# Cluster-ordered attention for the last batch of a routing-attention and PReLU feed-forward kernel

## The chip, the cores and the metric

One core of one Trainium2 chip runs the whole kernel. The metric is device microseconds of an execution, the median of three runs. Engines: TensorE (PE; PEld loads its weights), VectorE (DVE), ScalarE (ACT), GpSimd (POOL), SyncE (SP, which here only issues DMAs).

## The reference

```python
batch, n_heads, seq, head_dim = (4, 8, 768, 64); n_clusters = 16
q_assign = argmax(q_n . c_n);  k_assign = argmax(k_n . c_n)      # per head
mask = q_assign[:, :, :, None] == k_assign[:, :, None, :]
scores = where(mask, q @ k.T / sqrt(D), -1e9)
attn = softmax(scores)                                           # fp32
x = (attn @ v) as (B*S, H*D) = (3072, 512)
h = x @ w_in                                                     # (512, 2048)
g = maximum(h, 0) + alpha * minimum(h, 0)                        # alpha per column, random in 0..0.3
out = g @ w_out                                                  # (2048, 512)
```

A query attends only to keys of its own cluster. w_in, w_out and alpha arrive as 64-bit floats and are converted on the chip. Everything else is fp32.

## The kernel before, in words

**Tiling.** Two heads of a batch form a pair n (4 pairs a batch, 16 in all), a half is 384 of the 768 queries. Keys come in 6 chunks of 128. A step is one third of (pair, half): 3 steps a half, 12 for the four pairs of a half (UB), 96 in all (NS). The order is batch, half, pair.

**Attention.** `load` (L105) and `load_v` (L127) fetch a pair, in 32-element blocks, so that `prep_blocks` (L346) can turn it with VectorE block transposes into features by tokens. `prep_sims` (L362, TensorE) and `prep_argmax` (L372, VectorE) find the cluster of each token, `prep_clusters` and `prep_queries` (L407, L432) spread it into the layout that the mask needs. `score` (L470) multiplies each key chunk with the half's 384 queries for both heads: the two heads use 64 rows of the array each and run side by side (L484). ScalarE takes exp (L502, L505), and `mask` (L513) multiplies by "query's cluster equals key's cluster" with a VectorE operation of two inputs. Batch 0 is masked by an extra matmul instead. `add_up`, `turn`, `rows_sums`, `total` and `invert` (L523 to L569) build the softmax denominators: sums over chunks and a block transpose on VectorE, then a tiny matmul (L551) and a reciprocal. `weigh` (L571) multiplies values with E (L594), the two heads in two column halves; `normalise` (L617) writes xT, features by tokens.

**Feed-forward.** `ffn_pieces` (L628) cuts a half of a batch into 28 pieces: 16 `hidden` (four matmuls of 384 columns, L645, then two Relus on ScalarE, L652 and L653, and one VectorE operation L637) and 12 `final` (four matmuls of 512 columns, L665). The y of three token tiles are added on VectorE (L673) or copied on ScalarE (L671) and leave by SP (L676).

**Order.** The program order is written out by hand; each engine runs its own instructions in that order and waits for the others' semaphores. From step 24 on (L793) a step consists of slots. At the first step of a half, `score`, `invert`, `weigh` and `normalise` of the half before come first; then each slot runs one entry of `todo` (masks, sums), some feed-forward pieces of the half of a batch whose attention is complete (`feed`), and what `prep_at` has put there. `later(k, ...)` runs a piece k slots on. At the end the queue of pieces is emptied (L860): the feed-forward of the last half of batch 3 has no attention beside it. One piece is held back (L813, L837) to lie under the last `normalise`.

**Buffers.** The loads use `inp`, four tiles; small matmul results use one PSUM bank (`misc`, L79); feed-forward results and the two heads of a lone score chunk use two PSUM banks of `ps_f`; the exponentials have 9 E tiles after `more_room` (L465), which reuses the conversion's raw tiles. Weights are converted in steps up to 24, with GpSimd operations (L264). After that GpSimd has nothing to do.

**Check and slow path.** At the end a flag tells whether the softmax, which subtracts no maximum, stayed in range (L847 to L862). If not, `general` computes everything again. With these inputs it isn't run.

Of the kernel before, what the change touches and what calls it, by code (L numbers as in the profile page):

```python
# [8 lines left out]

FP32 = mybir.dt.float32  # L10
BF16 = mybir.dt.bfloat16
U32 = mybir.dt.uint32
# [9 lines left out]
def kernel(  # L22
# [21 lines left out]
    SCALE = float(D) ** -0.5  # L44
    GROUP = 2
# [16 lines left out]
    raws = fast.enter_context(tc.tile_pool(name="raws", bufs=1))  # L62
    cvt = fast.enter_context(tc.tile_pool(name="cvt", bufs=3))
# [5 lines left out]
    tpool = fast.enter_context(tc.tile_pool(name="tpool", bufs=2))  # L69
# [5 lines left out]
    fast.enter_context(tc.manual_schedule())  # L75

# [22 lines left out]
    pairs = [(b, hp) for b in range(B) for hp in range(NCH)]  # L99
    NP = len(pairs)  # L100
# [109 lines left out]
    def prepare_constants():  # L210
# [5 lines left out]
        for h in range(2):  # L216
# [7 lines left out]
        alpha_neg = const.tile([P, NF], FP32, name="alpha_neg")  # L224
        nc.vector.tensor_scalar(out=alpha_neg, in0=aps[:, 0:NF], scalar1=-1.0,
                                scalar2=None, op0=ALU.mult)
        return cT, alpha_neg
# [144 lines left out]
    def prep_argmax(n, ps):  # L372
# [15 lines left out]
        nc.vector.tensor_reduce(out=first, in_=top, axis=AX.X, op=ALU.max)  # L388
        firsts[n] = first
        if n >= NCH:  # L390
            return
        nc.vector.tensor_tensor(
            out=top, in0=top, in1=first[:, :, None].broadcast_to((P, 2 * NX, NC)),
            op=ALU.is_equal)
        member = fsp.tile([P, 2, HS], BF16, name="member")
# [36 lines left out]
    def prep_queries(n, half, h):  # L432
# [3 lines left out]
        if n < NCH:  # L436

            if h == 0:
# [12 lines left out]

    SB = NJ // GROUP
    assert NJ == GROUP * SB and SB == GT
    steps = [(b * NCH + hp, half, s)
             for b in range(B) for half in range(2)
             for hp in range(NCH) for s in range(SB)]
    NS = len(steps)
# [6 lines left out]

    def more_room():  # L465
        for raw in raw_tiles:
            e_tiles.insert(0, raw.rearrange("p n w -> p (n w)").bitcast(FP32)[
                :, 0:2 * HS].rearrange("p (h q) -> p h q", h=2))

    def score(n, half, chunks, alone=None):  # L470
# [7 lines left out]
        def bank(ps, h):  # L478
            return (ps[h] if isinstance(ps, list) else ps[:, h, :])[:, 0:HS]

        for c, ps in zip(chunks, pss):
            for h in range(2):
                r = h * D
                nc.tensor.matmul(  # L484
                    out=bank(ps, h),
                    lhsT=qkT[r:r + D, S + c * P:S + (c + 1) * P],
                    rhs=qkT[r:r + D, half * HS:(half + 1) * HS], start=True,
                    stop=not early_mask)
# [528 lines left out]
```

## Time and profile before

| | |
|---|---|
| time, median of 3 runs | 1021.64 us (1021.16 to 1021.64) |
| profiled execution | 1021.76 us, span 1019.6 us, clock 0.996 |
| DVE, busiest group L518 (masks) | 88.6 + 71.2 us |
| POOL after 175 us | nothing |
| DMA | 43.09 MB, mean 42 GB/s |

A group's row gives the line, engine and operation, out<-in by the program's names, partitions x elements, type and count; then the busy time in all, the mean ns of one, and the idle time just before them with the engine and line that ended it. A matmul row starts with the rows*columns of the array that it uses. An fp32 matmul of the source is two records. Two matmuls on different halves of the array overlap, and busy time counts the overlap once. The rows of stretches give start:end, length, then for each engine its busy time and count, the granted clock of TensorE, the DMA share and GB/s.

### The profile page before, as it was taken

How to read it: one execution, taken by the hardware profiler on the slowest of the kernel's cores; microseconds unless marked ns; L12 is line 12 of the kernel's file. 1: busy time of each engine (PE TensorE's matmuls, PEld its weight loads, DVE VectorE, ACT ScalarE, POOL GpSimd, SP SyncE). 2: the span in 40 equal slices, each digit the busy share in tenths (PEclk: the TensorE clock that was granted, in tenths of full speed). 3: DMA queues.
4: the chain of work that ended last, by engine and by line, in shares of the span. 5: the costliest groups of instructions: out<-in, count | busy, mean ns of one | idle time of the engine just before them, and what ended most of it. 6: DMA issues, size and time to landing. Idle time of an engine off the chain costs nothing.

```text
span 1019.6 us, 10615 instructions
## 1 busy us (share of the span) xinstructions
PE 998.6 (98%) x4067; PEld 491.3 (48%) x4067; DVE 671.5 (66%) x1185; ACT 325.0 (32%) x620; POOL 50.4 (5%) x71
## 2 busy tenths in 40 slices
PE   8899999999999999999999999999999999999997
PEld 5434444444454544545454454545445454544453
DVE  5887798588474776868667665878856585762111
ACT  5655544223230323313132232313323141321120
POOL 2323222000000000000000000000000000000000
PEclk9999999999999999999999999999999999999999
DMA  6533664030000232040000240213000000000000
GB/s 246 195 106 107 150 140 46 16 78 1 0 1 21 41 47 47 1 85 8 1 1 11 52 47 16 31 37 57 1 0 1 32 1 0 1 11 21 1 0 34
DMA packets 106122, 43.09 MB, mean 42 GB/s; under 512 B 95360, under 2 KB 98896, under 8 KB 106064
## 3 DMA queue, kind: packets, MB, share of 16 engines
q1 hardware_dynamic: 105216, 41.95, 18.0%
q8 instruction: 34, 0.56, 0.2%
q10 hardware_dynamic: 848, 0.39, 0.2%
q14 instruction: 24, 0.20, 0.1%
HBM read 35.69 MB, written 6.29 MB: 41 GB/s over the span
## 4 chain that ended last, share of the span: by engine, by line
PE 91%; DVE 4%; ACT 2%; DMA 1%; issue 1%; POOL 0%; ACTq 0%; DVEq 0%; POOLq 0%
PE fps L665 32%; PE fps L645 32%; PE vps L594 11%; PE sps L484 9%; PE fps L484 4%; PE mps L366 1%; PE sps L494 1%; ACT E L505 1%; ACT member L400 1%; DMA aq<-member 1%; PE mps L551 0%; ACT power L252 0%; PE fps L339 0%; PE fps L587 0%; DVE gT L637 0%
## 5 line engine op out<-in xcount | busy, mean ns | idle before, releaser
L645 PE MATMUL fps<-xT,w_in_sb 128*128 128x384 f32 x1024 | 342.4, 490 | 0.0
L665 PE MATMUL fps<-w_out_sb,gT 128*128 128x512 f32 x768 | 337.9, 595 | 1.1 <-DVE gT L637 1.1
L645 PEld LDWEIGHTS fps<-xT,w_in_sb 128*128 128x128 f32 x1024 | 190.8, 190 | 141.3 <-ACT raw L502 4.9
L665 PEld LDWEIGHTS fps<-w_out_sb,gT 128*128 128x128 f32 x768 | 143.9, 190 | 174.0 <-issue 161.1
L652 ACT ACTIVATE gT<-fps 128x384 f32<-128x384 f32 x128 | 62.9, 491 | 272.6 <-PE fps L645 272.6
L637 DVE SCALAR_TENSOR_TENSOR gT<-neg,alpha_neg,gT 128x384 f32<-128x384 f32 x128 | 80.6, 636 | 100.2 <-ACT neg L653 99.5
L518 DVE SCALAR_TENSOR_TENSOR raw<-aq,key,raw 128x384 f32<-128x384 bf16 x160 | 88.6, 613 | 35.0 <-ACT raw L505 23.1
L484 PE MATMUL sps<-qkT 64*128 64x384 f32 x576 | 110.9, 504 | 0.7 <-ACT E L505 0.7
L505 ACT ACTIVATE E<-sps 128x768 f32<-128x768 f32 x88 | 67.2, 813 | 71.4 <-PE sps L494 42.2
L518 DVE SCALAR_TENSOR_TENSOR E<-aq,key,E 128x384 f32<-128x384 bf16 x128 | 71.2, 613 | 19.2 <-ACT E L505 12.8
L594 PE MATMUL vps<-E,vt 128*64 128x384 f32 x448 | 82.9, 498 | 0.0
L484 PEld LDWEIGHTS sps<-qkT 64*128 64x128 f32 x576 | 52.0, 188 | 52.2 <-issue 20.9
L529 DVE TENSOR_TENSOR acc<-acc,E 128x768 f32<-128x768 f32 x64 | 61.2, 956 | 17.1 <-ACT E L505 15.3
L673 DVE TENSOR_TENSOR y<-y,fps 128x512 f32<-128x512 f32 x30 | 20.6, 686 | 74.5 <-PE fps L665 74.5
L653 ACT ACTIVATE neg<-fps 128x384 f32<-128x384 f32 x128 | 62.0, 484 | 0.1
L505 ACT ACTIVATE raw<-sps 128x768 f32<-128x768 f32 x56 | 42.9, 813 | 55.3 <-PE sps L484 55.2
L671 ACT COPY y<-fps 128x512 f32<-128x512 f32 x24 | 14.1, 586 | 135.5 <-PE fps L665 135.5
L594 PE MATMUL vps<-raw,vt 128*64 128x384 f32 x320 | 56.5, 491 | 0.0
L594 PEld LDWEIGHTS vps<-E,vt 128*64 128x64 f32 x448 | 29.6, 138 | 41.4 <-issue 41.1
L529 DVE TENSOR_TENSOR acc<-acc,raw 128x768 f32<-128x768 f32 x48 | 45.9, 955 | 1.0
L484 PE MATMUL fps<-qkT 64*128 64x384 f32 x192 | 41.5, 508 | 0.0
L502 ACT ACTIVATE raw<-fps 128x384 f32<-128x384 f32 x48 | 21.0, 493 | 59.2 <-PE fps L484 59.2
(99 smaller groups left out, 618.9 us busy)
## 6 DMA issues: line engine op xcount, KB each, us to landing
raw<-in_moe_w_in_dram SPq DMA_DIRECT2D x16, 512.0 KB, 4.5
raw<-in_moe_w_out_dram SPq DMA_DIRECT2D x16, 512.0 KB, 3.6
vt<-in_v_dram SPq DMA_DIRECT2D x16, 384.0 KB, 4.3
out_dram<-y SPq DMA_DIRECT2D x24, 256.0 KB, 2.0
qk<-in_q_dram SPq DMA_DIRECT2D x48, 96.0 KB, 3.8
qk<-in_k_dram SPq DMA_DIRECT2D x48, 96.0 KB, 3.6
qk<-in_q_dram SPq DMA_DIRECT2D x4, 384.0 KB, 5.4
qk<-in_k_dram SPq DMA_DIRECT2D x4, 384.0 KB, 5.9
```

The lines of the kernel that those rows point to most:

```text
L484: nc.tensor.matmul(out=bank(ps, h), lhsT=qkT[r:r + D, S + c * P:S + (c + 1) * P], rhs=qkT[r:r + D, half * HS:(half + 1) * HS], start=True, ...
L502: nc.scalar.activation(out=E[:, h, :], in_=ps[h][:, 0:HS], func=AF.Exp, scale=SCALE)
L505: nc.scalar.activation(out=E, in_=ps[:, :, 0:HS], func=AF.Exp, scale=SCALE)
L518: nc.vector.scalar_tensor_tensor(out=E[:, h, :], in0=aqs[n, half][:, h, :], scalar=keys[n][:, NJ + c, h:h + 1], in1=E[:, h, :], op0=ALU.is ...
L529: nc.vector.tensor_tensor(out=acc, in0=acc if first is None else first[3], in1=E, op=ALU.add)
L594: nc.tensor.matmul(out=po[r:r + D, 0:HS], lhsT=vts[n][:, h, c, :], rhs=e[:, h, :], start=(c == 0), stop=(c == NJ - 1))
L637: nc.vector.scalar_tensor_tensor(out=gs[f], in0=neg, scalar=alpha_neg[:, f:f + 1], in1=gs[f], op0=ALU.mult, op1=ALU.add)
L645: nc.tensor.matmul(out=ps[:, 0:HS], lhsT=w_in_sb[:, c, f * P:(f + 1) * P], rhs=xT[:, c, :], start=(c == 0), stop=(c == NCH - 1))
L652: nc.scalar.activation(out=gs[f], in_=ps[:, 0:HS], func=AF.Relu)
L653: nc.scalar.activation(out=neg, in_=ps[:, 0:HS], func=AF.Relu, scale=-1.0)
L665: nc.tensor.matmul(out=ps[:, 0:DM], lhsT=gs[f][:, i * P:(i + 1) * P], rhs=w_out_sb[:, f, :], start=on and f == f0, stop=off and f == f0 + ...
L673: nc.vector.tensor_tensor(out=ys[i], in0=ys[i], in1=ps[:, 0:DM], op=ALU.add)
```

## The change

- The last batch (n = 12 to 15) is no longer done in halves; its pairs take three steps each, so 84 steps instead of 96 (`steps += [(n, None, s) ...]`).
- Ahead of that, at steps 30, 36, 54 and 60 (`ORDERS`), a pair's queries and keys are loaded and turned, their clusters found (`order_sims`, `order_counts`), each token's running number in its cluster counted with a scan, and its place in cluster order worked out (`order_begins`, `order_ranks`).
- One entry a slot (`sorting`), q, k and v of 64 tokens at a time go through a stage tile and are scattered by GpSimd's indirect DMA as rows of 512 bytes to DRAM, q and, apart from them, k beside v, in cluster order: 12 scatters a head, 24 a pair, and 18 loads of stage tiles by SP. The token's number goes along with q. `order_load` reads the sorted rows back, four steps before use.
- In cluster order, a key chunk c is multiplied only with the query tiles c-1, c and c+1 (`window`). The sums over chunks (`add_near`), the weighing (`weigh_near`) and the masks take the same windows. The second half's product uses the misc bank.
- Way back: `normalise_near` writes features by sorted tokens; six TensorE transposes (`to_rows`) give rows, 12 indirect DMAs a pair put rows of 256 bytes to their tokens' places in DRAM (`put_back`), `fetch_back` reads them in blocks and `turn_back` turns them into xT, all spaced by slots.
- Both halves of the last batch's feed-forward follow at the end; 4 pieces are held back at the end of the steps 60 to 71 and 10 at the end of 72 to 83 (`kept`).
- PReLU: one ScalarE copy, then VectorE's max(alpha * h, h), in place of two Relus and h+ - alpha * h-. This holds for alpha up to 1, which is tested at the end.
- Also at the end: a test that each cluster's queries lie within the windows; if one fails, `general` runs.
- Memory: the conversion's tiles are freed at step 24 (`second_part`), five E tiles, the order's tiles and a third xT tile take their place. The sorted blocks, the tile before the way back and the one after it all come from `inp`'s four tiles.

```diff
+    def order_features(n, w):
+        us[n, w] = inp.tile([P, 2, NJ, D], FP32, name="qk").rearrange("p h j d -> p (h j d)")
+        nc.vector.transpose(out=us[n, w],
+                            in_=raw_qk.pop((n, w)).rearrange("p h j d -> p (h j d)"))
...
+        top, first = argmax(ps)
+        only_first(top, first)
+        member = ordp.tile([P, HS], BF16, name="mine")
+        nc.vector.transpose(out=member, in_=top.rearrange("p t c -> p (t c)"))
+        count = asg.tile([P, HS], FP32, name="simT")
+        nc.vector.tensor_tensor_scan(count, member, member, 0.0, ALU.add, ALU.max)
+        us[n] = member, count
+    def order_begins(n):
+        member, count = us[n]
+        ps = misc()
+        for i, m in enumerate(("before", "within")):
+            nc.tensor.matmul(out=ps[:, i:i + 1], lhsT=sorts[m], rhs=count[:, HS - 1:HS],
+                             start=True, stop=True)
+        later(1, lambda: order_ranks(n, ps))
...
+        nc.vector.tensor_tensor(out=begin, in0=ps[:, 0:2], in1=sorts["shift"], op=ALU.add)
+        nc.vector.tensor_copy(out=sorts["begins"][:, n - NO:n - NO + 1], in_=ps[:, 0:1])
+        nc.vector.scalar_tensor_tensor(out=count, in0=count, scalar=begin[:, 1:2],
+                                       in1=member, op0=ALU.add, op1=ALU.mult)
+        by_token = ordp.tile([P, NX, 2, NC], FP32, name="by_token")
+        nc.vector.transpose(out=by_token.rearrange("p x h c -> p (x h c)"), in_=count)
+        nc.vector.tensor_reduce(out=rank, in_=by_token, axis=AX.X, op=ALU.add)
+        nc.vector.tensor_scalar(out=off, in0=rank, scalar1=0.0, scalar2=float(2 * S - 1),
+                                op0=ALU.max, op1=ALU.min)
+        whole = tc.dram_tile([2 * 2 * S, P], FP32, name=f"scratch{n}")
+        scratch[n] = whole, dram_disjoint_views(whole, 2 * NX)
+        for i in range(2 * PARTS + STAGES):
+            if i >= STAGES:
+                for x in range(NX // PARTS):
+                    sorting.append(lambda i=i - STAGES, x=x: order_scatter(n, i, x))
+            if i < 2 * PARTS:
+                sorting.append(lambda i=i: order_stage(n, i))
+        later(1, lambda: order_clusters(n, begin))
...
+    def order_stage(n, i):
+        h, part = divmod(i, PARTS)
+        rows = slice(part * S // PARTS, (part + 1) * S // PARTS)
+        for src, p0, d0 in ((q, 0, 0), (k, TS, 0), (v, TS, D)):
+            nc.sync.dma_start(out=t[p0:p0 + TS, :, d0:d0 + D],
+                              in_=src[b, head, rows].rearrange("(x p) d -> p x d", p=TS))
...
+    def order_scatter(n, i, x):
+                in_=sorts["number"][0:TS, part * m:(part + 1) * m])
+        nc.gpsimd.indirect_dma_start(
+            out=scratch[n][1][h * NX + xx],
+            out_offset=bass.IndirectOffsetOnAxis(ap=ranks[n][:, xx, h:h + 1], axis=0),
+            in_=sorts["stage"][i % STAGES][:, x, :], in_offset=None,
+            element_offset=h * 2 * S * P)
...
+        for w in range(2):
+            raw = inp.tile([P, 2, NJ, D], FP32, name="qk")
+            for h in range(2):
+                r0 = (2 * h + w) * S
+                for x in range(D // Q):
+                    r = h * D + x * Q
+                    nc.sync.dma_start(
+                        out=raw.rearrange("p h j d -> p (h j d)")[r:r + Q, :].rearrange(
+                            "p (t i) -> p t i", i=Q),
+                        in_=whole[r0:r0 + S, x * Q:(x + 1) * Q].rearrange(
+                            "(t p) i -> p t i", p=Q))
...
+    def order_blocks(n, w):
+        nc.vector.transpose(
+            out=qkTs[n][:, w * S:(w + 1) * S],
+            in_=raw_qk.pop((n, w)).rearrange("p h j d -> p (h j d)"))
...
+             for b in range(WHOLE) for half in range(2)
              for hp in range(NCH) for s in range(SB)]
+    steps += [(n, None, s) for n in range(NO, NP) for s in range(SB)]
+    assert NJ == 6 and GROUP == 2
+    def window(c):
+        return max(0, c - 1), min(NJ, c + 2)
+    def shared(c, side):
+        lo, hi = window(c)
+        a, z = max(lo, side * HJ), min(hi, (side + 1) * HJ)
+        return (slice((a - side * HJ) * P, (z - side * HJ) * P),
+                slice((a - lo) * P, (z - lo) * P))
...
-        def bank(ps, h):
-            return (ps[h] if isinstance(ps, list) else ps[:, h, :])[:, 0:HS]
+        def bank(ps, h, m=HS):
+            return (ps[h] if isinstance(ps, list) else ps[:, h, :])[:, 0:m]
+        def queries(c):
+            lo, hi = ((half * HJ, (half + 1) * HJ) if half is not None else window(c))
+            return slice(lo * P, hi * P), (hi - lo) * P
         for c, ps in zip(chunks, pss):
+            tokens, m = queries(c)
             for h in range(2):
                 r = h * D
                 nc.tensor.matmul(
-                    out=bank(ps, h),
+                    out=bank(ps, h, m),
                     lhsT=qkT[r:r + D, S + c * P:S + (c + 1) * P],
-                    rhs=qkT[r:r + D, half * HS:(half + 1) * HS], start=True,
-                    stop=not early_mask)
+                    rhs=qkT[r:r + D, tokens], start=True, stop=not early_mask)
         if early_mask:
...
+    def add_near(n, side, E):
+        first, middle, third, across = ((0, 1, 2, 3), (5, 4, 3, 2))[side]
+        acc = accs[n, side] = accp.tile([P, 2, HS], FP32, name="acc")
+        for c in (first, across):
+            to, of = shared(c, side)
+            nc.vector.tensor_tensor(out=acc[:, :, to], in0=E[middle][:, :, to],
+                                    in1=E[c][:, :, of], op=ALU.add)
+        to, of = shared(third, side)
+        nc.vector.tensor_tensor(out=acc[:, :, to], in0=acc[:, :, to],
+                                in1=E[third][:, :, of], op=ALU.add)
...
+    def weigh_near():
+        n = waiting[0][0]
+        E = {c: e for _, _, c, e in waiting[:NJ]}
+        del waiting[:NJ]
+        for side in range(2):
+            po = pos[n, side] = (ps_v.tile([P, 512], FP32, name="vps") if side == 0
+                                 else misc())
+            for c in ((1, 0, 2, 3), (4, 5, 2, 3))[side]:
+                to, of = shared(c, side)
+                for h in range(2):
+                    r = h * D
+                    nc.tensor.matmul(out=po[r:r + D, to], lhsT=vts[n][:, h, c, :],
+                                     rhs=E[c][:, h, of], start=c in (1, 4), stop=c == 3)
+    def normalise_near(n):
+        outT = inp.tile([P, 2, NJ, D], FP32, name="qk").rearrange("p h j d -> p (h j d)")
+        for side in range(2):
+                                    in0=pos.pop((n, side))[:, 0:HS],
+                                    in1=rds.pop((n, side)), op=ALU.mult)
+        whole = tc.dram_tile([2 * S, D], FP32, name=f"back{n}")
+        nc.vector.tensor_scalar(out=place, in0=found[:, :, :, 0], scalar1=0, scalar2=S - 1,
+                                op0=ALU.max, op1=ALU.min)
+        rows = sorts["byrow"].tile([P, NJ, P], FP32, name="rows")
+        for i in range(2):
+            later(4 + 2 * i, lambda i=i: to_rows(outT, rows, i))
+        for i in range(2 * NJ):
+            later(8 + i // 2, lambda i=i: put_back(to, place, rows, i))
+        later(8 + NJ, lambda: fetch_back(n, whole))
+    def to_rows(outT, rows, i):
+        ps = misc()
+        for j in range(HJ):
+            nc.tensor.transpose(out=ps[:, j * P:(j + 1) * P],
+                                in_=outT[:, (i * HJ + j) * P:(i * HJ + j + 1) * P],
+                                identity=ident)
+        later(1, lambda: nc.scalar.copy(
+            rows[:, i * HJ:(i + 1) * HJ].rearrange("p j d -> p (j d)"), ps[:, 0:HS]))
+    def put_back(to, place, rows, i):
+        j, h = divmod(i, 2)
+        nc.gpsimd.indirect_dma_start(
+            out=to[i],
+            out_offset=bass.IndirectOffsetOnAxis(ap=place[:, h, j:j + 1], axis=0),
+            in_=rows[:, j, h * D:(h + 1) * D], in_offset=None, element_offset=h * S * D)
...
+    def fetch_back(n, whole):
+        raw = inp.tile([P, 2, NJ, D], FP32, name="qk").rearrange("p h j d -> p (h j d)")
+        for h in range(2):
+            for x in range(D // Q):
+                r = h * D + x * Q
+                nc.sync.dma_start(
+                    out=raw[r:r + Q, :].rearrange("p (t i) -> p t i", i=Q),
+                    in_=whole[h * S:(h + 1) * S, x * Q:(x + 1) * Q].rearrange(
+                        "(t p) i -> p t i", p=Q))
+        def turn_back():
+            for half in range(2):
+                if (b, half) not in xTs:
+                    pool = sorts["xmore"] if half else xpool
+                    xTs[b, half] = pool.tile([P, NCH, HS], FP32, name="xT")
+                nc.vector.transpose(out=xTs[b, half][:, hp, :],
+                                    in_=raw[:, half * HS:(half + 1) * HS])
+        later(4, turn_back)
...
+            while fresh:
+                f = fresh.popleft()
                 nc.vector.scalar_tensor_tensor(
-                    out=gs[f], in0=neg, scalar=alpha_neg[:, f:f + 1], in1=gs[f],
-                    op0=ALU.mult, op1=ALU.add)
+                    out=gs[f], in0=gs[f], scalar=alpha[:, f:f + 1], in1=gs[f],
+                    op0=ALU.mult, op1=ALU.max)
             gs[f] = gpool.tile([P, HS], FP32, name="gT")
-            nc.scalar.activation(out=gs[f], in_=ps[:, 0:HS], func=AF.Relu)
-            nc.scalar.activation(out=neg, in_=ps[:, 0:HS], func=AF.Relu, scale=-1.0)
-            negs.append((f, neg))
+            nc.scalar.copy(gs[f], ps[:, 0:HS])
+            fresh.append(f)
             if f % FQ == FQ - 1:
...
+    ORDERS = [30, 36, 54, 60]
+        if half is None:
+            t = ORDERS[n - NO]
+            load_at.setdefault(t - 1, []).append(lambda n=n: load(n))
+            for i in range(2):
+                at(t, FIRST + i, lambda n=n, i=i: order_features(n, i))
+            at(t + 1, FIRST + 1, lambda n=n: order_sims(n))
+            at(t + 2, FIRST, lambda n=n: order_begins(n))
+            load_at.setdefault(u - 4, []).append(lambda n=n: order_load(n))
+            at(u - 3, FIRST, lambda n=n: prep_clusters(n))
+            for i in range(2):
+                at(u - 2, FIRST + i, lambda n=n, i=i: order_blocks(n, i))
+                at(u - 1, FIRST + i, lambda n=n, i=i: order_queries(n, i))
+            continue
         if half == 0:
             if n < NCH:
...
+    def kept(block):
+        return {NS // UB - 2: 4, NS // UB - 1: 10}.get(block, 0)
...
-            weigh(GROUP if u == TOGETHER else NJ)
+            if prior[1] is None:
+                invert(prior[0], 1)
+                weigh_near()
+            else:
+                invert(*prior)
+                weigh(GROUP if u == TOGETHER else NJ)
...
-            normalise(*prior)
+            if prior[1] is None:
+                normalise_near(prior[0])
+            else:
+                normalise(*prior)
...
+            if half is None:
+                of = {c: e for _, _, c, e in E}
+                todo += [lambda n=n, E=of: add_near(n, 0, E),
+                         lambda n=n: (turn(n, 0), rows_sums(n, 0)),
+                         lambda n=n, E=of: add_near(n, 1, E),
+                         lambda n=n: (total(n, 0), turn(n, 1), rows_sums(n, 1)),
+                         lambda n=n: invert(n, 0)]
+                todo += [lambda: None] * 3 + [lambda n=n: total(n, 1)]
+            else:
...
+        if u == ORDERS[0] - 2:
+            order_constants()
...
-            pieces = len(ffn) - (NS - u <= UB) + -whole * left // (UB // SB * FREE)
+            pieces = len(ffn) - kept(u // UB) + -whole * left // (UB // SB * FREE)
             todo.popleft()()
+            if sorting:
+                sorting.popleft()()
             feed(max(pieces, 0))
...
     while due:
         tick()
+        if due:
+            tick()
+        feed(1)
```

## The prediction

> **What bounds the kernel now.** I read the busy totals first, then the stretches of the last batch, then the groups of the lines that the change edits.
>
> ```profile
> PE 998.6 (98%) x4067; PEld 491.3 (48%) x4067; DVE 671.5 (66%) x1185; ACT 325.0 (32%) x620; POOL 50.4 (5%) x71
> ...
> PE 91%; DVE 4%; ACT 2%; DMA 1%; issue 1%; POOL 0%; ACTq 0%; DVEq 0%; POOLq 0%
> ```
> TensorE has work 98% of the span and is 91% of the chain that ended last. So a change pays what it takes off TensorE, unless it opens a gap there. The stretches (span, then PE, PEld, DVE, ACT, POOL busy) show where a gap could open:
>
> ```profile
> 327.00:446.00 119.00, 119.00 (x449) 58.62 (x448) 86.09 (x145) 34.29 (x69) 0.00 (x0) 1.00 0.22 37
> ...
> 691.00:811.00 120.00, 120.00 (x454) 59.08 (x454) 84.20 (x147) 34.90 (x72) 0.00 (x0) 1.00 0.08 17
> 811.00:931.00 120.00, 118.56 (x432) 58.42 (x428) 74.82 (x126) 31.85 (x64) 0.00 (x0) 1.00 0.02 7
> 931.00:1019.60 88.60, 82.87 (x226) 42.56 (x226) 12.68 (x25) 15.70 (x35) 0.00 (x0) 0.99 0.03 10
> ```
> Twelve steps take 120 us, all TensorE; VectorE has some 35 us to spare in each twelve. The last batch's attention is 691 to 931, its last half's feed-forward the rest. The same stretches, of L484 (scores) and L594 (weighing) alone, hold per twelve steps (96 records):
>
> ```profile
> 327.00:446.00 119.00, 17.64 (x96) 8.60 (x96) 1.00 0.22 37
> ...
> 327.00:446.00 119.00, 16.36 (x96) 6.54 (x96) 1.00 0.22 37
> ```
> A source matmul is two records. A half of a pair is 24 records a line: 4.41 us of scores, 4.09 of weighing, 8.50 together.
>
> ```profile
> L645 PE MATMUL fps<-xT,w_in_sb 128*128 128x384 f32 x1024 | 342.4, 490 | 0.0
> L665 PE MATMUL fps<-w_out_sb,gT 128*128 128x512 f32 x768 | 337.9, 595 | 1.1 <-DVE gT L637 1.1
> L551 PE MATMUL mps<-part,fold 128*128 128x24 f32 x56 | 8.6, 233 | 2.8 <-DVE part L541 1.8 <-ACT every L417 1.0
> L653 ACT ACTIVATE neg<-fps 128x384 f32<-128x384 f32 x128 | 62.0, 484 | 0.1
> ```
> A feed-forward piece is 8 records: hidden 342.4/128 = 2.68 us, final 337.9/96 = 3.52 us; a tiny fp32 matmul (L551) is 8.6/28 = 0.31 us.
>
> [...] First GpSimd, then VectorE, in order of time:
>
> ```profile
> 79.06 1.40 POOL L264 TENSOR_TENSOR w_out_sb<-w_out_sb,power 128x512 f32<-128x512 f32 x1 [1.23 <-DVE w_out_sb L261]
> ...
> 79.23 1.50 DVE L248 TENSOR_SCALAR w_out_sb<-raw 128x512 uint32<-128x512 uint32 x1
> ...
> 82.92 0.42 DVE L246 TENSOR_SCALAR power<-raw 128x512 uint32<-128x512 uint32 x1
> ```
> L248 needs 0.42 us (as its twin L246 does) and took 1.50, to just after GpSimd's end; the two-input L637, 0.62 in the median, reached 1.64 in the worst case. [...] The kernel before issues no DMA from GpSimd[...]; SP's output DMAs here land 2.0 us after issue.
>
> **The change part by part**, against the profiled run (span 1019.6, time 1021.76, so 2.2 around it; 0.1 above the median).
>
> (1) Scores and weighing. A key tile now meets 2 or 3 query tiles, 2+3+3+3+3+2 = 16 of 36. Before: 8 halves x 8.50 = 68.0 us. After: 68.0 x 16/36 = 30.2. [...] 56 records a pair[...]. Between 0 and 3.1 us a pair (all 56 at 0.19, the mean load); I take 0.4, so 1.6. Saved: 36.2.
>
> (2) Added on TensorE. Way back: 24 transposes of 128x128; the nearest row, L339, is 0.07 us a record, so 0.07 to 0.29; I take 0.15: 3.6 us. Cluster beginnings: 8 tiny matmuls x 0.31 = 2.5. Span test: 4 x 0.31 = 1.2. Sum 7.3 (5.4 to 10.7). The similarities move 35 to 14 steps forward, the cluster numbers one step nearer their use; as many as before: 0. TensorE net: 36.2 - 7.3 = **-28.9**.
>
> (3) ACT copy for two Relus, alpha for its negative. L653 goes, 62.0 us of ACT, off the path (ACT is 32% busy, and no wait of TensorE is put down to L653); L637 stays one two-input operation. 0. If h times alpha were above h for negative h (alpha over 1) the slow path would run; the largest alpha is 0.2995.
>
> (4) Sorting on VectorE. Per pair, before: two transposes of 0.94 and 2.6 of maxima. After, in steps 30-33, 36-39, 54-57 and 60-63: those, then comparison 0.56, transpose 0.58, a scan (no row; 0.4 to 1.2, I take 0.8), ranks 2.3, clusters 1.5: 10.3, and the two transposes again later. 6 us more per pair under 30 us or more to spare: 0. The constants at step 28 go back and forth between VectorE and GpSimd; with what else is late by a slot I put **+1** (0 to 3).
>
> (5) Scatters. 24 a pair, 96 in all, on a GpSimd that is idle from 175 us on, one a slot (2.5 us); pair 12 from step 33 to 40 and read at 68, pair 15 to 71 and read at 77. They hide unless one takes over about 4 us (24 x 4 = 96 us in 7.5 steps of 10, a lag of 20, which is the lead of the loads below). SP gets some 42 DMAs a pair (8 loads, 18 stage loads, 12 reads of sorted rows, 4 of the way back) for 9. At 0.56 us an issue (four loads in 2.24 us) that is 24 us in 75. A stage load waits for the four scatters before it; behind it on SP stand the next pairs' loads, which are called two steps (20 us) ahead of use and land in 3.8, and the outputs. Each wait is 2 to 3 us: 0.
>
> (6) Steps 72 to 83, the closest race. TensorE: 22 feed-forward pieces (12 hidden, 10 final) 67.4; scores 4 x 4.0; weighing 4.1 for the old pair and 3 x 4.1; way back, sums, clusters 7: **107 us**. VectorE for a middle pair: masks 8 x 0.56 + 4 x 0.43 = 6.2, sums of E 3.6, turn and row sums 3.9, two inversions 3.4, normalising 1.3, blocks and queries of the next pair 4.3, turning back 1.2, slopes and y 2.2: 26; with the shorter first and last pairs **97 us**. Both are near 26.7 a pair, and each waits for the other: row sums (TensorE's L551 twin), the second reciprocal ahead of the second half's weighing (both hold the one misc bank), masks. Following one pair in order, the sums arrive 0.5 us late to 2 us early. I take **+3** (0 to 8).
>
> (7) The end. After the last weighing 10 pieces cover the way back: 4 x 2.68 + 6 x 3.52 = 31.8, 35 with the transposes and tests between. Under it: normalise, first transposes and copy 5.5; 12 row scatters in GpSimd's order at p each; landing 2.5; SP's four loads 5.5 (issue 2.2, landing); turn 1.2: 14.7 + 12 p. It hides to p = 1.7. I take p = 1.3 (0.6 to 2.5): 0. The present gap around the last flag, 1.3 us of the last stretch, gets the same cover: **-1.2**.
>
> Sum: 1019.6 - 28.9 + 1 + 3 - 1.2 = 993.5; with 2.2 around it 995.7, less 0.1: **995.6**.
>
> **The rivals.** (B) The way back shows. p = 2.5: 44.7 against 35, so +10; and 30 us of scatters a pair against 26.7 lag by another 10: 1006 to 1016. For it: no row prices the scatter[...]. (C) [...] VectorE's two-input masks, sums and slopes wait c each time. Steps 72-83 hold 36 row scatters: from c = 0.29 VectorE passes TensorE. Steps 36-47 hold 38 scatters over 86 + 11 us of VectorE: it passes from 0.6. At c = 0.8 this eats 18 + 7 = 25 us, the whole gain; at c = 1.0, 26 + 15, so **1033**. For it: the 1.50 above; against: a scatter reads only 128 offsets. (D) Short matmuls cost as much as their weight loads: 3.1 instead of 0.4 a pair, +11: 1007. (E) The change does not do what it says because the span test fails and the general path runs after all else. From the inputs, the widest span of the last batch is 218 of 256 allowed, so I give it nothing.
>
> **How the numbers follow.** Forecast 0.62 (988 to 1001), B 0.16, D 0.07, C 0.13, and 0.02 that C's smaller form cancels the gain. A run of this kernel can tell 0.2%, 2 us. Faster 0.62 + 0.16 + 0.07 = 0.85, same 0.02, slower 0.13. The low end is TensorE net -32.4 and no stall (988), the high end most of B and D (1014); it holds about 0.8.
>
> **What would show it.** Right: the scores' and weighing's records of the last batch near 30 us in all; steps 72 to 83 in about 110 us, with TensorE idle 3; no gap before the first hidden piece of the last batch; a scatter every 1.3 us at the end. Wrong: VectorE's masks longer than 0.56 while GpSimd works (C); TensorE waiting for a DMA into the way back's tile (B); 56 records a pair near 10 us (D); gaps between 300 and 690 us (part 5).

## The result, and the profile after

The changed kernel takes 1014.56 us in the median (1013.4 to 1017.87), the kernel before 1021.4 beside it: 0.9939 of the time before, 95% interval 0.9915 to 0.9963. The forecast was 995.6 (988 to 1014). So it is faster, by 7 us and not by 26. The profiled execution took 1013.4 us, span 1011.6: 8.0 less than before. The busy totals and the chain of the page after:

```profile
PE 974.3 (96%) x3955; PEld 484.7 (48%) x3955; DVE 655.0 (65%) x1209; ACT 259.6 (26%) x468; POOL 214.0 (21%) x249
...
PE 84%; DVE 11%; ACT 2%; issue 2%; DMA 1%; ACTq 0%; DVEq 0%; POOL 0%; POOLq 0%
```

TensorE is busy 24.3 us less, but VectorE now has 11% of the chain (4% before). The span without PE's busy time was 21.0 us and is 37.3: 16.3 of the 24.3 were given back as idle time. The same stretches as before, columns as there:

```profile
327.00:446.00 119.00, 116.56 (x443) 56.95 (x442) 90.47 (x159) 27.88 (x52) 44.41 (x45) 0.99 0.29 66
691.00:811.00 120.00, 117.66 (x508) 62.28 (x507) 98.79 (x191) 28.38 (x58) 37.52 (x36) 1.00 0.24 47
811.00:931.00 120.00, 119.05 (x331) 60.68 (x330) 22.67 (x54) 12.98 (x27) 11.71 (x12) 1.00 0.07 20
931.00:1011.60 80.60, 74.28 (x199) 37.43 (x197) 10.72 (x17) 8.02 (x17) 0.00 (x0) 0.97 0.03 11
```

The reader is to see that the sort's stretch (the first) has lost 2.4 us of TensorE that was full before, though VectorE is busy only 90.5 of its 119. Who waited there is in TensorE's waits (us in total, times, longest):

```profile
PE mps L805 <- DVE begins L573: 12.0, 4, 4.8
...
PE fps L991 <- issue: 2.3, 1, 2.3
```

L805 is `total`, once in each of the four stages with a sort (a stage is the three steps of one pair and half). These 12.0 us and the one gap of 2.3 at 629 us are 14.3 of the 16.3. The groups show the second loss:

```profile
L973 PE MATMUL fps<-xT,w_in_sb 128*128 128x384 f32 x1024 | 347.8, 494 | 0.8 <-issue 0.8
L991 PE MATMUL fps<-w_out_sb,gT 128*128 128x512 f32 x768 | 340.2, 598 | 3.4 <-issue 2.3
...
L625 POOL DMA_INDIRECT scratch<-stage,off x96 | 104.8, 1092 | 291.8 <-DVE gT L965 125.8
...
L919 POOL DMA_INDIRECT back<-rows,place x48 | 49.2, 1026 | 129.7 <-ACT rows L914 116.3
```

The feed-forward matmuls are as many as before, and cost 5.4 (L973) and 2.3 us (L991) more. Stretches of 2 us around the longest stop say why (PEclk is the third number from the end):

```profile
606.00:608.00 2.00, 0.00 (x0) 0.00 (x0) 2.00 (x4) 0.00 (x0) 0.00 (x0) 1.00 0.00 0
608.00:610.00 2.00, 0.13 (x1) 0.16 (x1) 1.97 (x6) 0.00 (x0) 0.00 (x0) 0.52 0.00 0
610.00:612.00 2.00, 2.00 (x5) 1.39 (x6) 1.90 (x5) 0.00 (x0) 0.00 (x0) 0.50 0.03 8
...
614.00:616.00 2.00, 2.00 (x7) 0.83 (x7) 1.76 (x6) 0.48 (x1) 1.70 (x2) 0.77 0.19 66
```

The granted clock is 1.00 in all such stretches of the kernel before between 200 and 990 us. Here it falls to half at 362, 608 and 632 us, behind stops of 2.1, 4.8 and 2.3 us; one minus the clock, summed over the stretches, is 6.9 us. The run with the sort in two stages, below, has the same instructions and lost no clock there: its TensorE is busy 967.5 us. So: work off TensorE -31.1 (998.6 to 967.5), half clock +6.8 (967.5 to 974.3), idle +16.3: the -8.0.

How a stop comes about, in the timeline of the stage of steps 60 to 62 (start, duration, engine, line, then the wait):

```profile
598.49 0.85 PE L544 MATMUL mps<-qk,cT 128*32 128x384 f32 x8
...
599.27 5.43 PE L973 MATMUL fps<-xT,w_in_sb 128*128 128x384 f32 x16
599.41 0.58 DVE L379 STREAM_TRANSPOSE simT<-mps 128x384 f32<-128x384 f32 x1 [1.61 <-PE mps L544]
...
603.40 0.96 DVE L557 TENSOR_TENSOR_SCAN simT<-mine 128x384 f32<-128x384 bf16 x1
...
604.54 0.54 PE L564 MATMUL mps<-simT,row 128*128 128x1 f32 x4
...
605.24 0.96 DVE L770 TENSOR_TENSOR acc<-acc,E 128x768 f32<-128x768 f32 x1
606.12 1.14 DVE L965 SCALAR_TENSOR_TENSOR gT<-gT,alpha 128x384 f32<-128x384 f32 x2
...
608.18 0.95 DVE L795 TENSOR_REDUCE part<-acc 128x24 f32<-128x768 f32 x1
...
609.58 0.14 DVE L573 COPY begins<-mps 128x1 f32<-128x1 f32 x1
...
609.87 0.59 PE L805 MATMUL mps<-part,fold 128*128 128x24 f32 x2 [4.79 <-DVE begins L573]
```

VectorE waits for the similarities, sorts from 599.4 to 604.3, and only then comes to the last sums, the slopes and the row sums (`part`, ready at 609.13). TensorE has just two hidden pieces (5.4 us) between the similarities and `total`. The wait is put down to the last reader of the misc bank (609.72), but `part` was only 0.6 us earlier. In the kernel before, the same place reads as follows in the stages of steps 30, 57 and 60:

```profile
292.39 0.95 DVE L541 TENSOR_REDUCE part<-acc 128x24 f32<-128x768 f32 x1
...
293.39 0.40 PE L551 MATMUL mps<-part,fold 128*128 128x24 f32 x2 [0.91 <-DVE part L541]
...
559.16 0.95 DVE L541 TENSOR_REDUCE part<-acc 128x24 f32<-128x768 f32 x1
...
565.66 0.30 PE L551 MATMUL mps<-part,fold 128*128 128x24 f32 x2
...
591.77 0.95 DVE L541 TENSOR_REDUCE part<-acc 128x24 f32<-128x768 f32 x1
...
593.29 0.30 PE L551 MATMUL mps<-part,fold 128*128 128x24 f32 x2
```

In the stage of step 60 `part` was ready at 592.72, 0.57 us ahead of its use. At step 30 VectorE was late already: TensorE waited 0.91 us for it. At step 57, where no sort was put, `part` was ready 5.55 us ahead. These lines were there to be read beforehand.

### The profile page after: what moved, and what is told of

Its sections match the earlier page's. It is cut to its first block, busy times and chain, and to the rows that moved or that the text cites. A ratio compares the mean times of both kernels' runs of the same rounds, so it can differ in the third digit from the quotient of the medians.

```text
span 1011.6 us, 10921 instructions
## 1 busy us (share of the span) xinstructions
PE 974.3 (96%) x3955; PEld 484.7 (48%) x3955; DVE 655.0 (65%) x1209; ACT 259.6 (26%) x468; POOL 214.0 (21%) x249
## 4 chain that ended last, share of the span: by engine, by line
PE 84%; DVE 11%; ACT 2%; issue 2%; DMA 1%; ACTq 0%; DVEq 0%; POOL 0%; POOLq 0%
PE fps L991 32%; PE fps L973 27%; PE vps L849 8%; PE sps L719 7%; PE fps L719 3%; DVE acc L770 1%; DVE gT L965 1%; PE sps L728 1%; PE mps L371 1%; PE vps L885 1%; DVE acc L789 1%; DVE more L760 1%; DVE E L760 1%; DVE part L795 1%; ACT E L740 1%
## 5 line engine op out<-in xcount | busy, mean ns | idle before, releaser
L973 PE MATMUL fps<-xT,w_in_sb 128*128 128x384 f32 x1024 | 347.8, 494 | 0.8 <-issue 0.8
L991 PE MATMUL fps<-w_out_sb,gT 128*128 128x512 f32 x768 | 340.2, 598 | 3.4 <-issue 2.3
L973 PEld LDWEIGHTS fps<-xT,w_in_sb 128*128 128x128 f32 x1024 | 192.2, 192 | 140.9 <-issue 11.6
L991 PEld LDWEIGHTS fps<-w_out_sb,gT 128*128 128x128 f32 x768 | 144.2, 191 | 178.2 <-issue 168.1
L625 POOL DMA_INDIRECT scratch<-stage,off x96 | 104.8, 1092 | 291.8 <-DVE gT L965 125.8
L965 DVE SCALAR_TENSOR_TENSOR gT<-gT,alpha 128x384 f32<-128x384 f32 x128 | 80.3, 637 | 131.6 <-ACT gT L979 120.0
L979 ACT COPY gT<-fps 128x384 f32<-128x384 f32 x128 | 61.2, 478 | 364.6 <-PE fps L973 342.2
L719 PE MATMUL sps<-qkT 64*128 64x384 f32 (+1 forms) x512 | 96.5, 494 | 0.8 <-ACT E L740 0.8
L760 DVE SCALAR_TENSOR_TENSOR more<-aq,key,more 128x384 f32<-128x384 bf16 (+1 forms) x136 | 74.5, 603 | 24.2 <-ACT more L740 16.8
L740 ACT ACTIVATE E<-sps 128x768 f32<-128x768 f32 (+1 forms) x81 | 61.2, 801 | 78.0 <-PE sps L728 44.4
L919 POOL DMA_INDIRECT back<-rows,place x48 | 49.2, 1026 | 129.7 <-ACT rows L914 116.3
L760 DVE SCALAR_TENSOR_TENSOR E<-aq,key,E 128x384 f32<-128x384 bf16 (+1 forms) x104 | 57.1, 602 | 11.9 <-ACT E L740 6.7
L740 ACT ACTIVATE more<-sps 128x768 f32<-128x768 f32 (+1 forms) x47 | 35.6, 796 | 40.2 <-PE sps L719 33.7
L849 PE MATMUL vps<-more,vt 128*64 128x384 f32 x220 | 38.8, 491 | 0.0
```

What stands on the lines that cost most here:

```text
L625: nc.gpsimd.indirect_dma_start(out=scratch[n][1][h * NX + xx], out_offset=bass.IndirectOffsetOnAxis(ap=ranks[n][:, xx, h:h + 1], axis=0), ...
L719: nc.tensor.matmul(out=bank(ps, h, m), lhsT=qkT[r:r + D, S + c * P:S + (c + 1) * P], rhs=qkT[r:r + D, tokens], start=True, stop=not early_ ...
L740: nc.scalar.activation(out=E[:, :, 0:m], in_=ps[:, :, 0:m], func=AF.Exp, scale=SCALE)
L760: nc.vector.scalar_tensor_tensor(out=e, in0=of, scalar=keys[n][:, NJ + c, h:h + 1], in1=e, op0=ALU.is_equal, op1=ALU.mult)
L849: nc.tensor.matmul(out=po[r:r + D, 0:HS], lhsT=vts[n][:, h, c, :], rhs=e[:, h, :], start=(c == 0), stop=(c == NJ - 1))
L919: nc.gpsimd.indirect_dma_start(out=to[i], out_offset=bass.IndirectOffsetOnAxis(ap=place[:, h, j:j + 1], axis=0), in_=rows[:, j, h * D:(h + ...
```

## The experiments

Theory 1: VectorE comes late to the row sums, because the sort stands ahead of them in a stage that has no time for it. Rivals: the one misc bank, held by `order_begins`; GpSimd's scatters, which would hold VectorE up or whose DMAs would hold loads up; the reads of the sorted rows.

**The bank.**

```diff
-            at(t + 2, FIRST, lambda n=n: order_begins(n))
+            at(t + 3, FIRST, lambda n=n: order_begins(n))
```


> Only order_begins moves, from two steps after the sort's start to three (the next stage's third slot), so that nothing of the sort holds the one misc bank when total (L805) wants it. Theory 1, VectorE late: total also waits for part (L795), which ended only 0.45 to 0.5 us ahead of the read of the bank (L573) in all four places; so each of the four stops shrinks by about 0.5 us and no more, 1 to 2 us in all: 1012 to 1014. Rival, the bank: the four stops (12.0 us) go, and the halved clock behind them with it: 996 to 1003.

Measured: 1009.57 us, ratio 0.9889 (0.9872 to 0.9905). The four stops stayed, 2.75, 1.99, 1.99 and 4.57 us, now put down to `part` (L795). The bank was worth 0.7 us in all. The time fell by more than expected because half the clock loss was absent in the profiled run (3.4 for 6.9 us) and the gap at 629 us did not come: chance, as the stretches on the clock below show.

**The scatters.** In `order_ranks` the calls of `order_stage` and `order_scatter` are left out, and `order_load` reads q, k and v in place of the scratch, with the rows' own numbers in place of `found`:

```diff
-            if i >= STAGES:
-                for x in range(NX // PARTS):
-                    sorting.append(lambda i=i - STAGES, x=x: order_scatter(n, i, x))
-            if i < 2 * PARTS:
-                sorting.append(lambda i=i: order_stage(n, i))
```


> The 96 sorting scatters and their 72 stage loads left out; the last batch's q, k and v are read in their own order from the inputs, in the same small packets (so the sorting itself is left out, all of its VectorE and TensorE work stays, and the way back keeps its scatters). Theory 1: the four stops stay as they are, only the gap at 629 us (2.3, and some clock) can go: 1009 to 1014. Rival, [...] their DMAs hold up loads: 8 us or more below the changed kernel, under 1006.

Measured: 1011.54 us, 0.9905 (0.9888 to 0.9921). Its first wait of TensorE is the same as with the scatters:

```profile
PE mps L798 <- DVE begins L573: 12.0, 4, 4.8
```

So the rival falls. VectorE shows no stretching either: a mask of 128x384 between 330 and 446 us has a mean of 614 ns before (L518), 612 in the changed kernel (L760), 612 without the scatters. Between 200 and 690 us of the changed kernel, 63 such masks ran beside a scatter (612 ns, the longest 680) and 129 did not (611 ns). A lengthening like that of L248 beside GpSimd's operation at 79 us of the kernel before (1.50 us for 0.42) is not seen beside these scatters.

**The reads of the sorted rows**, over three steps:

```diff
-            load_at.setdefault(u - 4, []).append(lambda n=n: order_load(n))
+            for part in range(3):
+                load_at.setdefault(u - 4 + part, []).append(
+                    lambda n=n, part=part: order_load(n, part))
```


> order_load split over three steps (found and queries, keys, values), so that the twelve reads of the sorted rows do not follow each other on SP. If the burst of small packets makes the gap at 629 us (all engines idle, 2.3 us on TensorE, and the low clock after it), the gap goes: 1010 to 1012. If it is something else: as the changed kernel, 1013 to 1015.

Measured: 1014.49 us, 0.9923 (0.9907 to 0.994). The gap at 629 us is gone, but a like one of 1.15 us stood at 316, and no other run had one at 629; so this run settles nothing about it.

**The sort over two stages.**

```diff
-            load_at.setdefault(t - 1, []).append(lambda n=n: load(n))
+            load_at.setdefault(t - 3, []).append(lambda n=n: load(n))
-                at(t, FIRST + i, lambda n=n, i=i: order_features(n, i))
-            at(t + 1, FIRST + 1, lambda n=n: order_sims(n))
-            at(t + 2, FIRST, lambda n=n: order_begins(n))
+                at(t - 1, SLOTS - 1, lambda n=n, i=i: order_features(n, i))
+            at(t, FIRST, lambda n=n: order_sims(n))
+            at(t + 3, FIRST, lambda n=n: order_begins(n))
```


> The sort spread over two stages: features at the end of the stage before, similarities a step and a slot earlier, beginnings and ranks in the next stage. The same work on every engine. Theory 1, VectorE late by the sort just ahead of the row sums: the counts now lie at the start of a stage, ten slots ahead of the row sums, and the four stops go (-12), the half clock behind three of them too (-5 to -7): 995 to 1001. Rival, [...] the scatters are as many, so the lateness stays: above 1008.

Measured: 1001.83 us, 0.9808 (0.9792 to 0.9825). Two stops are gone, two of 2.7 us stay (steps 30 and 60), with no clock lost in the profiled run (997.94 us; the other three took 1001.8 to 1002.8). Right in direction, just outside the range: the stages of steps 30 and 60 have six hidden pieces and 25.2 us of TensorE work, the other two seven and 27.8, and in the shorter ones even the sort's first half makes `part` late.

**Another kind of stage.** A stage holds some 7 pieces: 7 hidden, or 1 hidden and 6 final, which last 5 to 9 us longer. In the kernel before, between 300 and 660 us, `part` is ready 0.6 to 0.8 us ahead of `total` in stages of the first kind and 5.5 to 7.6 us ahead in the second. All four sorts lay in stages of the first kind. Two were moved, two left:

```diff
-    ORDERS = [30, 36, 54, 60]
+    ORDERS = [33, 36, 57, 60]
```


> The sorts of the pairs 12 and 14 start at steps 33 and 57 in place of 30 and 54; those of 13 and 15 stay at 36 and 60. Theory 1, sharpened to the stage: a stage of 7 hidden pieces lasts 25.4 to 26.8 us in the kernel before and its VectorE is busy 18.9 to 20.3, one of 1 hidden and 6 final pieces lasts 32 to 34.5 with VectorE busy 19; the sort adds 7.5 to 9 us, more than the 6.5 to 7 to spare in the first kind and less than the 12 to 15 in the second. So the stops of the moved pairs (3.0 and 2.1 us) go with the half clock behind them, and those at 36 and 60 (2.1 and 4.8) stay: 1006 to 1010, with two stops left. Rival, what follows the sort (scatters, loads, the bank) wherever it lies: four stops, 1013 to 1016.

Measured: 1001.49 us, 0.9803 (0.9787 to 0.9819). The four stages with a sort, in this run:

```profile
297.10:333.00 35.90, 35.90 (x128) 16.61 (x126) 28.88 (x50) 5.51 (x11) 1.18 (x1) 1.00 0.24 52
333.00:363.60 30.60, 28.50 (x120) 14.93 (x118) 27.82 (x52) 7.93 (x16) 21.54 (x24) 1.00 0.38 92
543.50:576.80 33.30, 33.30 (x120) 15.09 (x118) 28.34 (x49) 5.01 (x10) 1.86 (x2) 1.00 0.26 58
576.80:610.00 33.20, 28.41 (x114) 14.87 (x112) 29.22 (x55) 7.47 (x15) 25.40 (x29) 0.90 0.28 79
```

The same VectorE work of 28 to 29 us leaves TensorE full where a stage lasts 33 to 36 us anyway (first and third), and stops it by 2.1 and 4.8 us where TensorE has 28.5 us of work (second and fourth). The gain is larger than expected: TensorE is idle 8.1 us less than in the changed kernel (the two stops, the gap at 629 and small ones) and busy 4.6 less (3.4 of it are half of the clock loss).

**All four there, and begun early.** The edit of the two stages with `ORDERS = [33, 39, 57, 63]`, the constants kept at step 28, and `order_begins` at t + 1:

> All four sorts in the stages of final pieces (33, 39, 57, 63), the features at the end of the stage before, similarities at the start of the stage and the beginnings one step after. Theory 1: none of the four stops is left, nor the half clock behind them: 12.0 and about 6.7 us less than the changed kernel, 994 to 999, TensorE idle about 22 to 26 us in all. Rival: the same work and traffic still makes stops elsewhere, above 1003.

Measured: 995.63 us (994.88 to 996.08), 0.9743 (0.9727 to 0.976). The busy totals, and the wait that is left:

```profile
PE 968.0 (97%) x3955; PEld 482.6 (49%) x3955; DVE 655.0 (66%) x1209; ACT 258.4 (26%) x468; POOL 208.4 (21%) x249
```
```profile
PE mps L805 <- DVE part L795: 3.8, 3, 2.7
```

The same instructions as the changed kernel's in other places, and 18.9 us faster. The two profiled executions differ by 18.5 us; 4.0 of these are the gap at 629 us and the clock behind it (2.3 and 1.7), which the place of the sorts is not shown to have made. The other 14.5 go with the stops. The 2.7 us are the sort at 63: that stage has 4 us less of TensorE work than its twin at 57 (29.1 against 33.1), since pieces are kept for later.

**VectorE work alone**, in the kernel before, with nothing of the change:

```diff
+    def dose(times):
+        t = asg.tile([P, HS], FP32, name="simT")
+        nc.vector.memset(t, 0.0)
+        for _ in range(times):
+            nc.vector.tensor_tensor(out=t, in0=t, in1=t, op=ALU.max)
+    for t, times in ((30, 7), (36, 10), (54, 13), (60, 16)):
+        prep_at.setdefault((t + 1, SLOTS - 1), []).append(
+            lambda times=times: dose(times))
```


> The kernel before, and nothing of the change: only idle work for VectorE (7, 10, 13 and 16 maxima of 128x384 with themselves, 0.59 us apart, so 4.1, 5.9, 7.7 and 9.4 us) at the end of the second step of the stages that begin at steps 30, 36, 54 and 60. In the kernel before VectorE is idle some 3.0 us between that place and the row sums, and the row sums are ready 0.05 (stage 30) and 0.57 us (the others) ahead of total. Theory 1 (a stage of hidden pieces has so little to spare just there): stops at L551 of 1.0, 2.3, 4.1 and 5.8 us, 13 in all, and the half clock behind the longer ones: 1035 to 1046. If a stage's whole spare time (6.5 us) counted: 0, 0, 1.2 and 2.9: 1025 to 1029. By the prediction's own reading (30 us to spare in each twelve steps): no stop, 1021 to 1023.

Measured: 1055.47 us, 1.0336 (1.032 to 1.0352). TensorE's timeline at the four places:

```profile
293.45 0.62 PE L551 MATMUL mps<-part,fold 128*128 128x24 f32 x2 [2.66 <-DVE part L541]
...
362.19 0.62 PE L551 MATMUL mps<-part,fold 128*128 128x24 f32 x2 [5.66 <-DVE part L541]
...
552.75 0.62 PE L551 MATMUL mps<-part,fold 128*128 128x24 f32 x2 [7.44 <-DVE part L541]
...
622.52 0.62 PE L551 MATMUL mps<-part,fold 128*128 128x24 f32 x2 [9.22 <-DVE part L541]
```

A dose of k maxima takes 0.38 + 0.59 k: 4.5, 6.3, 8.1 and 9.8 us. From the second on, each stop is its dose less 0.6, which is the 0.57 us of `part` ahead of `total` in the kernel before. My expectation was too small: in these three places VectorE's idle time lies ahead of the dose (it waits for the slopes' inputs), and none of it could be used. In the first place 2.6 us of idle time lie behind the dose and take that much of it up: TensorE's wait, 0.9 us before, is 1.8 longer. The half clock came behind all four stops; TensorE, with the same work, is busy 7.1 us longer. So VectorE work alone makes the stops, with no scatter and no sorted load in the program, and the spare time that counts is neither a stage's nor twelve steps', but what lies between the added work and its deadline.

**The cover at the end**: eight pieces kept in place of ten (`NS // UB - 1: 8`).

> Eight pieces in place of ten kept for the end, so two final pieces (7.0 us) less lie over the way back. In the changed kernel the last transpose back ends at 834.96 us and the first piece that reads it starts at 839.84, 4.9 us later. If the last half's hidden pieces wait for the way back alone, TensorE now stops 2.1 us ahead of the first of them: 1016 to 1018. If something else shares that place or the way back is faster than the trace says: no stop, 1014 to 1015.

Measured: 1009.66 us, 0.988 (0.9863 to 0.9896): faster than the changed kernel, a miss on both sides. The end:

```profile
835.26 2.74 PE L973 MATMUL fps<-xT,w_in_sb 128*128 128x384 f32 x8
...
836.06 1.03 DVE L941 STREAM_TRANSPOSE xT<-qk 128x384 f32<-128x384 f32 x2
```

TensorE starts the piece before the last rows are turned back, with no stop: the last pair's rows are the fourth and last source that a hidden piece adds up, and its first six records do not read them. And the two pieces added to steps 72 to 83 cover waits that the changed kernel had there: 0.47, 0.95 and 0.38 us between 757 and 766 are gone. With these and the gap at 629 us, TensorE's idle time is 4.5 us less. Together with the early sorts:

> The sorts in the stages of final pieces, begun early, with eight pieces in place of ten kept for the end, so that the last twelve steps have two pieces more to cover attention. In the run with eight kept alone, the waits for ACT and for the row sums between 750 and 766 us (2.2 us) were gone and the end had no stop. Theory: 2 us less than the sorts early alone: 992.5 to 994.5. Rival: what eight kept pieces gained was only the gap at 629 us that the changed kernel's profile had once: 995 to 996.

Measured: 998.74 us, 0.9778 (0.9765 to 0.9792): 3.1 us slower than the early sorts alone, a miss. At 738 us TensorE stops 2.3 us for a ScalarE copy (L979) that starts at 739.80 although its input was complete at 736.08. Half clock follows, and also behind the stop of 2.7 us at 623, where the early sorts alone kept the full clock: 1.7 us each. Why that copy was late no view shows; the gap at 629 us in the changed kernel was of this kind, a copy at 630.80 for 629.05. Open. With `{NS // UB - 2: 2, NS // UB - 1: 8}`:

> As with early sorts and eight kept, and two pieces in place of four kept from the twelve steps before, so that the stage 63 to 65, which has 4 us less of TensorE work than its twin at 57, gets some of it back: the stop of 2.7 us at 623 us in the run with early sorts shrinks to under 1. Theory: another 1.5 to 2.5 us: 990.5 to 992.5. Rival: the two pieces are then missing in steps 72 to 83 and a stop opens there: as with eight kept.

Measured: 993.71 us (993.4 to 994.28), 0.9723 (0.971 to 0.9737): the fastest here, and 1.2 us above the expected range. The stop at the sort of step 63 is gone; but, as the rival foresaw, stops stand in steps 72 to 83: between 715 and 754 us they are 0.4 to 1.3 us long and 4.3 in all, where the early sorts alone had 2.0.

**The PReLU form alone**, in the kernel before:

```diff
-            nc.scalar.activation(out=gs[f], in_=ps[:, 0:HS], func=AF.Relu)
-            nc.scalar.activation(out=neg, in_=ps[:, 0:HS], func=AF.Relu, scale=-1.0)
-            negs.append((f, neg))
+            nc.scalar.copy(gs[f], ps[:, 0:HS])
+            fresh.append(f)
```


> The kernel before with nothing but the ACT copy and the maximum in place of the two Relus, without the test that the slopes are at most 1. ACT loses 62 us of work that no wait of TensorE is put down to: the same time as before, 1020.5 to 1022.5. Rival: part of the gain of the changed kernel comes from here, 1019 or less.

Measured: 1020.66 us against 1021.86, 0.9988 (0.9981 to 0.9995). ScalarE's busy time fell by 50.3 us (325.0 to 274.7; the two Relus of a piece overlapped by 0.1 us), and that bought 1.2.

## Why the prediction was wrong

- **(1) and (2) held.** Scores and weighing of the last batch were 35.3 + 32.7 = 68.0 us and are 16.3 + 14.7 = 31.0; forecast 68.0 to 31.8. The 31.0 are 0.8 above 16/36 of 68.0; the 1.6 that the forecast allowed there was my estimate. Transposes 4.1 (3.6), beginnings 2.1 (2.5), span test 0.4 (1.2). TensorE net -31.1, forecast -28.9. Rival D did not happen.
- **(3) held** within 1.2 us.
- **(4) is the step that failed**: "6 us more per pair under 30 us or more to spare: 0". Both numbers were wrong in kind. The 6 is 10.3 us of sort less some 4.5 that go away in other steps (and leaves out the two transposes that come again later, 1.9 us); in its own stage (from one stage's first weighing to the next's) VectorE gained 8.2, 9.1, 7.5 and 8.7 us. The 30 was an average over twelve steps of two kinds of stages; in the stages that the sort was put in, VectorE was busy 18.8 to 20.3 of 25.4 to 26.8 us; in three of them it was 0.57 us ahead of `total`, and in the first already late. The prediction's own row of L551 had that wait (1.8 us for L541, 0.9 of it at step 30). The scan took 0.96 us (L557), against 0.8 that rested on no row. What came of it: 12.0 us of stops, and 6.8 us of half clock, of which the prediction had no term. Moving the sorts, without removing an instruction, gave 18.9 of the missing 19.0 us back, some 4 of them perhaps by chance (the gap at 629 us).
- **(5)** held: the 24 scatters of a pair, 1.09 us each, stayed hidden. The gaps between 300 and 690 us that were to show this step wrong came from (4).
- **(6)** was too dear: from the first weighing of step 72's stage to that of step 84's passed 101.8 us, forecast 110. The per-record sums of a group count overlapping records twice; TensorE was busy 99.5 us, while its groups sum to 104.
- **(7)** held: the twelve scatters in a row at the end start 1.28 us apart on average, so p = 1.28 against 1.3, which rested on no row.
- Rival B did not happen, nor C (a mask took 612 ns beside a scatter and 611 apart from one), nor E.

That the variant with all sorts moved lands on 995.63 is partly luck: (1) and (6) were cheaper than forecast, and a stop of 2.7 us is still in it.

## What to carry to other kernels

Work for a side engine is free only if it fits between the place where it is put and the next thing that the bounding engine takes from that engine: read, for that very stage, when the producer ended and when the consumer started. Stages of one loop can differ by a third in length (here 25.4 to 26.8 us and 32 to 34.5); average over one kind at a time, and do not net work that is added in one stage against work removed in another. A stop of the bounding engine can cost more than its length: here 6.8 us of half clock came on top of 14.3 us of stops.

## What was not expected of the hardware

After a stop TensorE ran at half its clock in many cases. Over all these profiles, between 200 us and the last matmuls, each of nine stops of 4.5 us or more was followed by it, 12 of 23 stops of 2.0 to 3.0 us, and none under 1.4 us. One minus the clock, summed over such an event, is mostly 1.7 or 3.4 us (half speed for 3.4 or 6.8 us). In each trace all stretches of half clock begin on one grid of 3.41 us: in the changed kernel at 362.33, 608.09 and 631.98 us, 72 and 7 pieces of it apart. What follows a stop of 2.0 to 3.0 us goes with where the grid cuts it. The stop of 2.73 us at the sort of step 63 stands in two runs, cut into pieces of the grid here (TensorE's busy time comes first, its clock is the third number from the end). With eight pieces kept:

```profile
622.59:626.00 3.41, 0.68 (x4) 0.51 (x4) 3.34 (x5) 0.00 (x0) 2.83 (x4) 1.00 0.11 38
626.00:629.41 3.41, 3.41 (x5) 1.36 (x5) 1.92 (x6) 0.00 (x0) 2.80 (x3) 0.50 0.34 95
```

With the early sorts alone:

```profile
620.89:624.31 3.42, 2.29 (x6) 0.74 (x4) 3.32 (x5) 0.00 (x0) 2.81 (x3) 1.00 0.11 38
624.31:627.72 3.41, 1.82 (x6) 1.09 (x7) 3.33 (x7) 0.00 (x0) 2.52 (x5) 1.00 0.11 38
627.72:631.13 3.41, 3.41 (x15) 1.46 (x14) 0.63 (x3) 1.02 (x2) 2.80 (x4) 1.00 0.51 116
```

In the first run one piece is idle for 0.80 of its length, and half clock follows; in the second the stop is split, 0.33 and 0.47, and nothing follows. Of the 32 stops, all 18 that left one piece idle for 0.61 of it or more were followed by half clock, three of nine between 0.49 and 0.57, and none of five below. In the changed kernel the stop of 2.10 us at 359 lay in one piece, 0.62 of it, and half clock followed; the one of 2.10 us at 545 was cut into 0.57 and 0.05, and nothing followed. What decides between 0.49 and 0.57 stays open. Whether the half clock makes the changed kernel's four runs lie 4.5 us apart is not shown: the fastest and the slowest, 1013.4 and 1017.87 us, both had a mean clock of 0.989. The five of the fastest variant, which has no stop over 1.4 us there, lie 0.9 apart, at 0.995 to 0.996.
